# Four unread 4 MB transfers, in rows of 32 KB, in the load stream of a decode kernel

## The chip, the cores and the metric

The kernel runs on one core of one Trainium2 chip. The metric is the device time of one execution in microseconds (us). The time of a kernel is the median of its runs; the profile shows one execution, whose own span is a little shorter than its time.

## What is computed

One decode step: attention over the last 2048 of 8192 cached keys, mixed by a gate with a small MLP. There are 8 batches (B), 16 key/value heads (Hkv), 32 query heads, a head size of 128, a model size of 576, and all data is bf16.

```python
def reference(A_x, A_k_cache, A_v_cache, A_wq, A_wo, B_x, B_w1, B_b1, B_w2, B_b2, gate_w):
    def _A_ref(x, k_cache, v_cache, wq, wo):      # caches: [8, 16, 8192, 128]
        ...
        W = min(4096, max(256, Sk // 4))          # 2048
        q = (x @ wq).reshape(B, Sq, Hq, Dh).transpose(0, 2, 1, 3)
        k = jnp.repeat(k_cache[:, :, Sk - W:, :], rep, axis=1)
        v = jnp.repeat(v_cache[:, :, Sk - W:, :], rep, axis=1)
        scores = jnp.einsum("bhqd,bhkd->bhqk", q, k) * (Dh ** -0.5)
        o = jnp.einsum("bhqk,bhkd->bhqd", _softmax(scores), v)
        return o.transpose(0, 2, 1, 3).reshape(B, Sq, Hq * Dh) @ wo
    def _B_ref(x, w1, b1, w2, b2):
        h = _gelu(_layernorm(x) @ w1 + b1)
        return h @ w2 + b2
    x = A_x
    g = _sigmoid((x * gate_w).sum(-1, keepdims=True))
    return g * _A_ref(...) + (1 - g) * _B_ref(...)
```

The part of the caches that counts is 8 x 16 x 2048 x 128 x 2 B x 2, or 134 MB. The weights add another 20 MB.

## The kernel before

The kernel is a stream of loads with work hung on each. For each of the 16 key/value heads there is one K tile and one V tile, 4 MB each: all 8 batches, 2048 keys, 128 elements. `load_item` (line 602) issues such a load. It writes 128 partitions with two rows of 16 KB each, and reads the cache with the keys in 32 pieces of 64 outside and the batches inside. One pair of batch and head has 8192 keys of 256 B in the cache, so 2 MiB; neighbouring batches of the same head lie 32 MiB apart.

The list `stream` (lines 573 to 581) gives the order: K0, K1, K2, then V0, K3, V1, K4 and so on, after every fourth V tile a chunk of A_wo (`wo_chunk`, line 721), and at the end the bias and two groups of chunks of B_w2 (`m2_chunk`, line 738). In this text K8 is the K tile of head 8. Before the stream, A_wq and B_w1 are loaded for the query projection and the MLP's first layer.

All loads of the stream are issued by SyncE, in the order of the list: each has the one before it as its `after`. There are four slots of 32 KB a partition (`slot`, line 346), which `take_slot` (line 597) hands out in turn; the chunks of A_wo have a smaller fifth. A load waits until its slot is free, that is, until the last reader of the tile that lay there four tiles ago has finished. For a K tile (`k_unit`, line 641) the readers are four transposes on VectorE (line 649), behind each of which eight score matmuls on TensorE follow (lines 661 and, for those that keep their weights, 175). For a V tile (`v_item`, line 673) the reader is its product with the probabilities on TensorE (line 683). Two heads form a group; after the second K tile of a group comes its softmax (`softmax`, line 619: maximum on VectorE, exponent on ScalarE, transposed probabilities on VectorE), after its second V tile an evaluation on VectorE (lines 693 and 696).

Each engine runs its own list of instructions in order. These lists are made at build time by a planner (`_Plan.schedule`, line 62), which places each ready operation at the earliest time it can start by assumed durations, with 428 GB/s for loads. So a longer stream can also reorder work on other engines.

```python
        def load_item(cache, nm, hkv):
            s = take_slot()
            src = cache[:, hkv, S0:Sk, :].rearrange("b (x r) d -> x b (r d)", x=32)
            d = dma("sp", lambda e: e.dma_start(slot(s).rearrange("p (u n) -> p u n", u=2), src), "s%d" % s, 8 * W * Dh * 2, deps=slot_free[s], name="%s%d" % (nm, hkv), after=last_dma[-1:])
```

Of the kernel before, what the change touches and what calls it, by code (L numbers as in the profile page):

```python
# [38 lines left out]
class _Plan:  # L39
# [16 lines left out]
    def dma(self, eng, fn, semkey, nbytes, deps=(), name=None, after=(), prio=0):  # L56
        op = _Op(eng, fn, deps, name, self.DMA_ISSUE, after=after, is_dma=True, dma_sem=semkey, nbytes=nbytes, prio=prio)
        op.idx = len(self.all)
        self.all.append(op)
        return op  # L60
# [121 lines left out]
def build_kernel(nc, A_x, A_k_cache, A_v_cache, A_wq, A_wo, B_x, B_w1, B_b1, B_w2, B_b2, gate_w, out):  # L182
    B, Sq, D = A_x.shape
    _, Hkv, Sk, Dh = A_k_cache.shape
    Hq = A_wq.shape[1] // Dh
    F = B_w1.shape[1]
    W = min(4096, max(256, Sk // 4))
    assert Sq == 1 and Dh == 128 and B == 8 and W == 2048 and Hq == 2 * Hkv and Hkv == 16
    assert D == 576 and F == 4608
    S0 = Sk - W  # L190
# [19 lines left out]
    with ExitStack() as es:  # L210
# [135 lines left out]
        def slot(s):  # L346
            return RAW[:, s * DE:min((s + 1) * DE, ND * DE + SE)]
# [8 lines left out]
        def col(i, parts=128):  # L356
# [17 lines left out]
        add, dma = P.add, P.dma  # L374
# [7 lines left out]
                   deps=[o_idf], name="r8", cost=0.2)  # L382
# [19 lines left out]
        dx = [d_x, d_gw, d_gw1]  # L402
# [10 lines left out]
        for s in range(2):  # L413
            o_xz.append(add("dve", (lambda s=s: lambda e: e.tensor_copy(xz[:, s, :].rearrange("p (k z) -> p k z", z=2)[:, :, s], x_sb[:, 512:576]))(),  # L414
                            deps=dx + [o_xz0], name="xz%d" % s, cost=0.12))
# [12 lines left out]
        for s in range(2):  # L428
            o_yz.append(add("dve", (lambda s=s: lambda e: e.tensor_copy(yz[:, s, :].rearrange("p (k z) -> p k z", z=2)[:, :, s], y_bf[:, 512:576]))(),
                            deps=[o_y, o_yz0], name="yz%d" % s, cost=0.12))  # L430
# [142 lines left out]
        stream = [("K", 0), ("K", 1), ("K", 2)]  # L573
        for vi in range(Hkv):
            stream.append(("V", vi))
            if (vi + 1) % NVW == 0:
                stream.append(("W", vi // NVW))
            if vi + 3 < Hkv:
                stream.append(("K", vi + 3))
        M_CUTS = [[12, 12], [8, 3, 1]]  # L580
        stream += [("B", 0)] + [("M", i) for i in range(len(M_CUTS))]

        last_dma = [d_w1r]
        slot_free = [[o_qp], [], [], [o_hp], [o_qp, o_hp]]
# [12 lines left out]
        def take_slot():  # L597
            n = n_slot[0]
            n_slot[0] += 1
            return (1, 2, 0, 3)[n % ND]  # L600
# [5 lines that stand above are left out]
            last_dma.append(d)  # L606
            slot_free[s] = []
            return s, d

        def query(g):  # L610
            qb_done[g] = []
            for a in range(4):
                def fn(e, a=a):
                    dst = bass.AP(arena, offset=32 * a * AST + aoffs("qbd") + 32 * a, ap=[[AST, 32], [520, 4], [128, 4], [1, 8]])
                    src = bass.AP(arena, offset=32 * a * AST + aoffs("q4") + 32 * g, ap=[[AST, 32], [8, 4], [256, 4], [1, 8]])
                    return e.tensor_copy(dst, src)  # L616
                qb_done[g].append(add("pool", fn, deps=o_q4 + [o_qz, qk_unit.get(4 * g - 1)], name="qr%d_%d" % (g, a), cost=0.4))
# [54 lines left out]

        def v_item(hkv):
            s, d = load_item(A_v_cache, "dv", hkv)
            i = 2 * hkv + 1
            g, q = divmod(i, 4)
# [61 lines left out]
        def m2_chunk(ci):  # L738
            s = take_slot()
            j = sum(sum(c) for c in M_CUTS[:ci])  # L740
            at = 0
            src = B_w2.rearrange("(p j) n -> p (j n)", j=FT)
            ops = []
            for n, jn in enumerate(M_CUTS[ci]):
                d = dma("sp", (lambda j=j, jn=jn, at=at: lambda e: e.dma_start(slot(s)[:, at * D:(at + jn) * D], src[:, j * D:(j + jn) * D]))(),
                        "t%d" % (sum(len(c) for c in M_CUTS[:ci]) + n), 128 * jn * D * 2, deps=slot_free[s] if n == 0 else [], name="d_w2_%d_%d" % (ci, n), after=last_dma[-1:])
                last_dma.append(d)
# [8 lines left out]
        def k_item(hkv):  # L756
            s, d = load_item(A_k_cache, "dk", hkv)
            for u in range(2):
                k_unit(2 * hkv + u, s, d)
# [8 lines left out]
        pv_hist = []  # L768
        query(0)
        for kind, i in stream:  # L770
            {"K": k_item, "V": v_item, "W": wo_chunk, "M": m2_chunk, "B": bias}[kind](i)

        acc_ops = [g_.op for g_ in acc_groups]
        fin = []
# [34 lines left out]
def bass_gated_mix__sliding_block_cached__mixer_channel_mlp__decode_kernel(  # L809
    nc: bass.Bass,  # L810
    A_x: bass.AP,
    A_k_cache: bass.AP,
    A_v_cache: bass.AP,
    A_wq: bass.AP,
    A_wo: bass.AP,
    B_x: bass.AP,
    B_w1: bass.AP,
    B_b1: bass.AP,
    B_w2: bass.AP,
    B_b2: bass.AP,  # L820
    gate_w: bass.AP,
    out: bass.AP,
):
    build_kernel(nc, A_x, A_k_cache, A_v_cache, A_wq, A_wo, B_x, B_w1, B_b1, B_w2, B_b2, gate_w, out)
# [28 lines left out]
```

## Time and profile before

| what | value |
|---|---|
| median of 2 runs | 367.08 us (366.44 to 367.72) |
| the profiled execution | 366.56 us, of which span 364.7 us |
| TensorE matmuls, busy | 242.6 us (67% of the span) |
| VectorE, busy | 217.3 us (60%) |
| ScalarE / GpSimd, busy | 39.9 us / 23.2 us |
| moved by the DMA engines | 154.48 MB, mean 424 GB/s |
| 16 loads of K, 4096 KB each, median from issue to landing | 28.0 us |
| 16 loads of V, 4096 KB each, median from issue to landing | 32.6 us |

"Busy" is the time an engine spends in instructions. Loads are issued on SyncE's queue ("SPq") and run on the core's 16 DMA engines; the page gives their busy share (DMA, which rounds to a little over 1 when they are full) and what they move in GB/s. PE is TensorE, DVE VectorE, ACT ScalarE, POOL GpSimd, PEld TensorE's weight loads. L649 is line 649 of the kernel. The chain of waits follows the execution back from its last instruction: at each step to whatever released it, or to the instruction before it on its engine.

### The profile page before, as it was taken

Reading aid. Unit: us, or ns where it says so; the run is one execution under the profiler, and the core shown is the slowest. Engines: PE = TensorE matmul, PEld = TensorE weight load, DVE = VectorE, ACT = ScalarE, POOL = GpSimd, SP = SyncE. Lnnn points to the kernel's source line nnn. Section 1 sums busy time; section 2 is a strip of 40 time slices with the busy share of each in tenths; the row PEclk is TensorE's granted clock in tenths of the full one; section 3 lists DMA queues with packets and bytes.
Section 4 is the critical chain, followed back from the end, with each engine's and each line's share of the span. In section 5 each row is a group of like instructions: output and inputs, shape, how many; then the busy total and the mean of one; then the engine's idle time right before and its main releaser. Section 6 shows DMA issues by size and latency. Waiting matters only on the chain.

```text
span 364.7 us, 2619 instructions
## 1 busy us (share of the span) xinstructions
PE 242.6 (67%) x1329; PEld 57.0 (16%) x893; DVE 217.3 (60%) x160; ACT 39.9 (11%) x46; POOL 23.2 (6%) x66
## 2 busy tenths in 40 slices
PE   0346566599397956859197956868197948686675
PEld 0100000122011121202011121202011220102232
DVE  0722999666884757266774657276766668284220
ACT  1012100400400040000400040000400040002000
POOL 7210001000100100001000100001000100000000
PEclk9985599699979976969778976969798976989699
DMA  8999999999999999999999999999999999999995
GB/s 348 432 410 429 431 431 431 431 431 430 429 431 431 429 428 431 433 431 433 429 431 431 433 431 429 431 433 431 431 429 431 426 431 429 431 431 431 426 437 244
DMA packets 10675, 154.48 MB, mean 424 GB/s; under 512 B 764, under 2 KB 932, under 8 KB 1320
## 3 DMA queue, kind: packets, MB, share of 16 engines
q1 hardware_dynamic: 10608, 154.29, 99.0%
q8 instruction: 9, 0.15, 0.1%
q10 hardware_dynamic: 56, 0.03, 0.0%
q14 instruction: 2, 0.02, 0.0%
HBM read 154.31 MB, written 0.01 MB: 423 GB/s over the span
## 4 chain that ended last, share of the span: by engine, by line
DMA 58%; DVE 22%; PE 15%; issue 2%; ACT 1%; ACTq 0%; POOL 0%; DVEq 0%
DMA arena<-in_A_k_cache_dram 49%; DVE arena L649 18%; PE ps L175 9%; DMA arena<-in_B_w_dram 7%; PE ps L661 2%; DMA arena<-in_gate_w_dram 2%; PE ps L683 2%; PE ps L486 1%; DVE arena L548 1%; DVE arena L622 1%; ACT ps L631 1%; PE ps L565 0%; ACT arena L522 0%; DVE arena L543 0%; DVE arena L506 0%
## 5 line engine op out<-in xcount | busy, mean ns | idle before, releaser
L649 DVE STREAM_TRANSPOSE arena<-arena 128x2048 f32<-128x2048 f32 x64 | 144.5, 2291 | 60.0 <-DMA arena<-in_A_k_cache_dram 38.6
L175 PE MATMUL ps<-arena 128*128 128x512 bf16 (+2 forms) x453 | 136.3, 457 | 39.7 <-DVE arena L649 36.6
L683 PE MATMUL ps<-arena 128*32 128x512 bf16 x512 | 60.3, 390 | 3.1 <-DVE arena L637 2.0
L661 PE MATMUL ps<-arena 128*128 128x512 bf16 x114 | 50.5, 443 | 17.7 <-DVE arena L649 17.7
L626 ACT ACTIVATE arena<-ps,arena 128x2048 bf16<-128x2048 f32 x8 | 15.7, 1967 | 239.5 <-DVE arena L625 239.5
L661 PEld LDWEIGHTS ps<-arena 128*128 128x128 bf16 x128 | 13.9, 109 | 171.0 <-DVE arena L649 113.5
L683 PEld LDWEIGHTS ps<-arena 128*32 128x32 bf16 x512 | 25.1, 99 | 46.6 <-issue 20.4
L622 DVE TENSOR_REDUCE arena<-ps 128x1 f32<-128x2048 f32 x8 | 18.3, 2286 | 12.5 <-PE ps L175 12.4
L616 POOL COPY arena<-arena 32x128 bf16<-32x128 bf16 x32 | 9.2, 287 | 212.7 <-PE ps L175 202.9
L633 DVE STREAM_TRANSPOSE arena<-arena 128x2048 bf16<-128x2048 bf16 x8 | 18.3, 2291 | 6.4 <-ACT arena L626 6.4
L693 DVE SCALAR_TENSOR_TENSOR arena<-ps,arena 128x512 f32<-128x512 f32 x8 | 6.0, 752 | 20.2 <-PE ps L683 20.2
L565 PE MATMUL ps<-arena 128*8 128x288 bf16 (+1 forms) x140 | 12.6, 339 | 7.1 <-DVE arena L708 5.8
L702 PE MATMUL ps<-arena 128*128 128x256 f32 x16 | 5.6, 431 | 16.0 <-POOL arena L698 16.0
L635 PE MATMUL ps<-arena 128*128 128x1 f32 x16 | 4.5, 353 | 15.1 <-ACT ps L631 14.3
L631 ACT ACTIVATE ps<-arena 128x2048 f32<-128x2048 f32 x7 | 13.1, 1875 | 0.1
L698 POOL TENSOR_TENSOR arena<-arena 128x256 f32<-128x256 f32 x8 | 4.9, 612 | 109.4 <-DVE arena L625 61.7
L440 PE MATMUL ps<-arena 8*128 8x8 bf16 x8 | 0.6, 171 | 14.7 <-DVE arena L414 9.6
L696 DVE TENSOR_REDUCE arena<-arena 128x128 f32<-128x512 f32 x8 | 8.4, 1047 | 0.3
L565 PEld LDWEIGHTS ps<-arena 128*8 128x8 bf16 (+1 forms) x140 | 6.4, 97 | 13.5 <-DVE arena L708 7.0
L705 ACT ACTIVATE arena<-ps,arena 64x256 bf16<-64x256 f32 x8 | 3.7, 464 | 42.9 <-PE ps L702 42.8
L708 DVE STREAM_TRANSPOSE arena<-arena 128x256 bf16<-128x256 bf16 x4 | 2.5, 632 | 9.8 <-ACT arena L705 9.8
L543 DVE TENSOR_TENSOR arena<-arena 128x1152 f32<-128x1152 f32 x1 | 1.4, 1359 | 11.3 <-ACT arena L541 11.3
(86 smaller groups left out, 64.5 us busy)
## 6 DMA issues: line engine op xcount, KB each, us to landing
arena<-in_A_k_cache_dram SPq DMA_DIRECT2D x16, 4096.0 KB, 28.0
arena<-in_A_v_cache_dram SPq DMA_DIRECT2D x16, 4096.0 KB, 32.6
arena<-in_B_w_dram SPq DMA_DIRECT2D x1, 4608.0 KB, 23.4
arena<-in_A_wo_dram SPq DMA_DIRECT2D x4, 1152.0 KB, 34.1
arena<-in_A_wq_dram SPq DMA_DIRECT2D x1, 4096.0 KB, 12.9
arena<-in_B_w_dram SPq DMA_DIRECT2D x2, 1728.0 KB, 27.7
arena<-in_B_w_dram SPq DMA_DIRECT2D x1, 1152.0 KB, 27.1
arena<-in_B_w_dram SPq DMA_DIRECT2D x1, 576.0 KB, 24.3
```

What stands on the lines that cost most here:

```text
L175: return e.add_instruction(mybir.InstMatmult(name=nc.get_next_instruction_name(), engine=mybir.EngineType.PE, ins=[e.lower_ap(rhs), e.lowe ...
L565: ins = e.matmul(ps[32 * j:32 * j + 8, BK_ACC, 0:JN], lhsT, rhs[:, JN * j:JN * j + JN], start=False, stop=True, skip_group_check=True, til ...
L616: return e.tensor_copy(dst, src)
L622: mx = add("dve", lambda e: e.tensor_reduce(out=k(MX), in_=ps[:, 0:4, :].rearrange("p a n -> p (a n)"), axis=AXL.X, op=ALU.max), deps=[qk_ ...
L626: ex = add("act", lambda e: e.activation(out=Pm, in_=ps[:, 0:4, :].rearrange("p a n -> p (a n)"), func=ACTF.Exp, bias=k(NB), scale=SCALE, ...
L631: mask_done[g + 1] = add("act", lambda e: e.activation(out=ps[:, 0:4, :].rearrange("p a (n c) -> p (a n) c", c=4), in_=bass.AP(arena_f, of ...
L633: pt_done[g] = add("dve", lambda e: e.transpose(bass.AP(arena, offset=aoffs("PT") + 2048 * (g % 2), ap=[[AST, 128], [8, 64], [512, 4], [1, ...
L649: tr = add("dve", (lambda h=h, kb=kb: lambda e: e.transpose(bass.AP(arena_f, offset=foffs("KT") + kb * 2048, ap=[[AST // 2, 128], [1, 2048]]),
L661: mm = e.matmul(*args, start=False, stop=True, skip_group_check=True) if rc == 0 else held_matmul(nc, e, *args, stop=True, skip=True)
L683: mm = e.matmul(ps[c:c + 32, BK_OS[g % 2], :], PT[:, g % 2, 16 * c + 32 * t:16 * c + 32 * t + 32], slot(s)[:, (j % 2) * SE + 512 * t:(j % ...
L693: vmul = add("dve", lambda e: e.scalar_tensor_tensor(out=vmv, in0=ps[:, BK_OS[g % 2], :].rearrange("p (r d) -> p r d", r=4), scalar=rr[:, ...
L696: acc_ev[g] = add("dve", lambda e: e.tensor_reduce(out=EV[:, g % 2, :], in_=vm.rearrange("p (r d) -> p d r", r=4), axis=AXL.X, op=ALU.add) ...
```

## The change

Behind the K tiles of heads 8 and 11 in the stream, two more transfers each take the next slots in turn. Each moves 4 MB of the same caches: 32 pairs of batch and head (pairs 0 to 31 in the first two transfers, 64 to 95 in the other two, from A_k_cache and A_v_cache alternately), of each pair the first 512 of the last 2048 keys. The 128 KB of a pair go to four neighbouring partitions as four rows of 32 KB, which follow one another in the cache; the next pair begins 2 MiB further on. No operation reads what they bring. The slot is handed on when the transfer has landed.

```diff
@@ -577,6 +577,8 @@
                 stream.append(("W", vi // NVW))
             if vi + 3 < Hkv:
                 stream.append(("K", vi + 3))
+            if vi in (5, 8):
+                stream += [("X", 2 * (vi // 6)), ("X", 2 * (vi // 6) + 1)]
         M_CUTS = [[12, 12], [8, 3, 1]]
         stream += [("B", 0)] + [("M", i) for i in range(len(M_CUTS))]
@@ -606,6 +608,13 @@
             last_dma.append(d)
             slot_free[s] = []
             return s, d
+
+        def spare_item(n):
+            s = take_slot()
+            src = (A_k_cache, A_v_cache)[n % 2].rearrange("b h s d -> (b h) s d")[64 * (n // 2):64 * (n // 2) + 32, S0:S0 + 512, :].rearrange("j (x r) d -> j x (r d)", x=4)
+            d = dma("sp", lambda e: e.dma_start(slot(s), src), "s%d" % s, 8 * W * Dh * 2, deps=slot_free[s], name="dx%d" % n, after=last_dma[-1:])
+            last_dma.append(d)
+            slot_free[s] = [d]
@@ -768,7 +777,7 @@
         pv_hist = []
         query(0)
         for kind, i in stream:
-            {"K": k_item, "V": v_item, "W": wo_chunk, "M": m2_chunk, "B": bias}[kind](i)
+            {"K": k_item, "V": v_item, "W": wo_chunk, "M": m2_chunk, "B": bias, "X": spare_item}[kind](i)
```

The four transfers are called X0 to X3 below. In the lists of the engines, SyncE has four loads of 128 x 16384 elements more, X0 and X1 between K8 and V6, X2 and X3 between K11 and V9. TensorE, VectorE, ScalarE and GpSimd have the same instructions as before; on TensorE the products of V6, V9 and V10 and on VectorE the evaluation of V9's group have moved back by one to four places, and on ScalarE the mask of the sixth group stands before an output step and not behind it.

## The prediction

> **What bounds the kernel now.** I read the page's slices of the span first, then the table of stretches, the chain of waits, the queue of SyncE, and the row of the cache loads. The slices, each a fortieth of the span (9.1 us):
>
> ```profile
> DVE  0722999666884757266774657276766668284220
> DMA  8999999999999999999999999999999999999995
> GB/s 348 432 410 429 431 431 431 431 431 430 429 431 431 429 428 431 433 431 433 429 431 431 433 431 429 431 433 431 431 429 431 426 431 429 431 431 431 426 437 244
> ```
>
> The DMA engines are full from the second slice to the last but one and stay between 410 and 437 GB/s, while VectorE, the busiest helper in the loop, has room in most slices (60% of the span, TensorE 67%). The stretches sharpen this; the columns are the stretch, its length, the busy time of each engine, the clock, the DMA share and GB/s:
>
> ```profile
> 5.00:10.00 5.00, 0.41 (x7) 0.39 (x7) 0.81 (x3) 0.00 (x0) 2.90 (x3) 1.00 1.01 435
> ...
> 22.00:27.00 5.00, 1.89 (x7) 0.41 (x5) 1.10 (x1) 1.47 (x8) 1.15 (x4) 0.68 0.86 360
> ...
> 357.00:360.80 3.80, 2.46 (x29) 1.00 (x28) 0.00 (x0) 0.00 (x0) 0.00 (x0) 1.00 0.93 387
> 360.80:364.70 3.90, 1.71 (x24) 0.89 (x24) 0.45 (x1) 0.40 (x1) 0.00 (x0) 1.00 0.15 52
> ```
>
> Only the ends and one stretch near 25 us have free DMA time. In the middle, a stretch that begins where one wait for a K tile ends and stops where such a wait ends two groups of heads later, has none:
>
> ```profile
> 195.73:276.25 80.52, 55.49 (x281) 12.64 (x188) 50.19 (x32) 8.59 (x8) 3.52 (x10) 0.83 1.01 431
> ```
>
> In 80.5 us go four K tiles, four V tiles and one chunk of A_wo: 8 x 4.194 MB + 1.180 MB = 34.73 MB, and 34.73 MB / 80.52 us = 431.4 GB/s. The other three such stretches last 80.69, 80.69 and 80.46 us, so 430.4 to 431.7. VectorE works 50.2 of the 80.5 us. In the chain of waits the pieces are the same: after its transposes VectorE stands on the next K tile (start, length, what):
>
> ```profile
> 206.15 31.25 DMA arena<-in_A_k_cache_dram
> ...
> 248.71 27.51 DMA arena<-in_A_k_cache_dram
> ```
>
> The first number is when that tile was issued, so the issue came about 30 us, three tiles of 9.7 us, before the landing: the queue was two tiles deep when it went in. The row of the cache loads has the least and the most time from issue to landing:
>
> ```profile
> DMA to landing us min/median/max: 18.9/31.4/43.6
> ```
>
> Even the least, 18.9 us, is twice the 9.7 us of one tile. So SyncE waits a lot for free slots (212 us on the transposes in its own list of waits), but its next tile is always in the queue before the last one is through. The kernel is bound by bytes at 431 GB/s, with some 9 us of it at the ends.
>
> **The change, part by part.** It adds four DMA issues on SyncE's queue, X0 and X1 behind K8, X2 and X3 behind K11. It removes nothing.
>
> Bytes: each carries 32 x 512 x 128 x 2 B = 4.194 MB, so four are 16.78 MB. At the stretch's 431 GB/s that is 16.78 MB / 431 GB/s = 38.9 us. Nothing hides it: the stretches on both sides of K8 and K11 have a DMA share of 1.01, and all that follows in the stream moves back by it.
>
> Rate: no row has this pattern of reading, 128 rows of 32 KB where four follow one another and the next four begin 2 MiB on (a pair holds 8192 keys of 256 B). The nearest rows differ in one property each. The main load of A_wq also has 32 KB rows on 128 partitions, but without gaps; it lies in the stretch from 5 to 10 us, 435 GB/s. The K and V tiles have 16 KB rows and go through eight batches 32 MiB apart before they step to the next keys; they run at 431. So neither the long row nor a large step between neighbouring rows is dear by itself. What is new is that the two come together with places 2 MiB apart read at the same time. For bounds I take the highest rate of any stretch that I read (442 GB/s, 14 to 22 us: 38.0 us) and the lowest in which the loop's tiles were moving (the 360 GB/s above, which holds idle time too: 46.6 us). I choose 431, from the rows with the large step, which are nearest in their addresses: 38.9 us, between 38.0 and 46.6.
>
> The Trainium skill, page DMA: Bandwidth & Descriptors, section Latency and other measured facts, has a rule against this: copies of 128 rows of 16 KiB between HBM tensors ran at 207 GB/s in each direction at a row pitch of 512 KiB, 164 at 2 MiB and 103 at 4 MiB, where a padded pitch gave 214. By its 2 MiB figure the estimate is 38.9 x 214 / 164 = 50.8 us, by its 512 KiB figure (the mean pitch of a row here, four to a pair) 40.3 us. The K tiles' 32 MiB steps at 431 GB/s do not bear the rule out in its plain form, and no run here shows the pitch in question.
>
> Issue: four times 0.60 us on SyncE (its issues of cache tiles last 601 to 692 ns), beside a queue two tiles deep: nothing.
>
> Waits of the new transfers: X0 waits for the product of V4 and X1 for the transposes of K7, which V6 and K9 wait for now, in the same places; behind them on SyncE stand V6, K9 and all later loads. The chain gives the landing of K7 as 156.7 us (a piece of 32.75 us from 123.96 on), so V5 lands near 166.5, K8 near 176.2, X0 near 185.9 and X1 near 195.7, tile by tile of 9.7. The issues of now tell when each slot is free: V6's at 153.6 becomes X0's, K9's at 167.4 X1's, V7's at 173.0 (V5's product done) V6's, K10's at 191.0 (K8's transposes done) K9's. At 191.0 X1 and V6 still fill the queue until 205.4, so 14 us of it are left. V7 and K10 now wait for X0 and X1 themselves to land, near 186 and 196; nobody reads those, so their slots come free without transposes, and at 196 the queue holds V6, K9, V7 and a chunk of A_wo. Behind K11 it goes the same way: K11 lands near 256.9, X3 near 276.4, and K12 comes when K11's transposes are through, 11.3 us after its landing as now (248.7 against 237.4), with two tiles queued. No gap, so 0; were the queue to run dry once behind each pair, the price is a start from empty: the first load of A_wq, 0.52 MB, needed 3.6 us to landing where 431 GB/s would move it in 1.2, so 2.4 us, twice, 4.8 us.
>
> Order on the engines: TensorE does the product of V6 one half-tile later (behind K8's last score half, data already there), those of V9 and V10 behind score or softmax work of tiles that land earlier, and VectorE puts V9's evaluation behind the softmax steps of the group before. None of these now waits for a later tile. All lies beside 19.5 us of transfers that bring TensorE and VectorE no work, twice: 0. The cover for it is the 30 of 80.5 us in which VectorE is free.
>
> The tail: 36 tiles in place of 32 leave the order of the four slots as it was at the end, so the last loads and the 3.9 us behind them stay: 0.
>
> Sum: the profiled execution took 366.56 us (span 364.7 and 1.9 around it); 366.56 + 38.9 = 405.5. The two times shown have a median of 367.08, 0.5 more; 367.08 + 38.9 = 406.0. I take 405.8.
>
> **The rivals.**
>
> *Reads that collide.* The DMA engines, reading pairs 2 MiB apart in step, meet in the same part of the memory, and the four transfers run below the rest. For it: the loop's own tiles keep the engines on neighbouring keys, so the trace has never tried this. Against it: 32 MiB steps at 431 GB/s, and 128 KB in a row at each place. Mild, from the 360 GB/s above to three quarters of 431 (323): 46.6 to 51.9 us, 413 to 418.5. Strong, half of 431: 77.9 us, 444.5. It decides from about 415 GB/s down, where the four last over 40.4 us. The skill's rule named above is this rival; its 2 MiB figure gives an estimate of 417.4, its 4 MiB figure 447.
>
> *The queue runs dry* behind each pair, because V7 and K10 wait for a transfer rather than for compute: 4.8 us more, 410.5. Against it are the three tiles queued at K10's issue.
>
> *Not slower.* The four transfers find room that the DMA engines have, beside K and V tiles that leave it unused; the place is the stretch from V5's landing to K13's. The free DMA time that the stretches show is 1.0 us before 5 us, 0.7 near 25, and 0.3 + 3.3 behind 357, together 5.3 us and none of it at that place. To stay within 2% (7.3 us) 16.78 MB would have to pass at 2,300 GB/s, over five times the highest rate seen; it decides only if the tiles' share there fell well below 1. Or the transfers don't move all they name; but four issues with 128 x 16384 elements stand in SyncE's order. Faster than before needs a gain beyond the 38.9 us, and the free time is only 5.3.
>
> **How the numbers follow.** Full rate, no gap: 0.66, 404 to 408 (442 GB/s at 404.6 less half a microsecond between executions; 415 GB/s and the higher median at 407.5). Queue dry: 0.08, near 410.5. Mild collision: 0.16, 413 to 418.5. Strong collision: 0.08. Not slower: 0.02. The range from 404 to 418 takes in the first three but for their edges, some 0.85; stopping short of the mild collision would leave out a quarter. Over 2%, which is about what a measurement of this kernel can tell from no change, lies at 374.4: slower has 0.98, within 0.015, faster 0.005.
>
> **What would show it.** In the changed profile: 171.3 MB in the queue of the loads; slices at 431 GB/s without a dip at the two places, about 176 to 196 us and 257 to 276 us; two stretches of some 19.5 us in which TensorE and VectorE have little to do; the chain's share of K loads up by about 39 us; an unchanged tail. A dip of the slices at a DMA share near 1 speaks for colliding reads; a dip with a lower share for a dry queue. The forecast is wrong if the four transfers together take under 37 or over 41 us of the DMA engines.

## The result, and the profile after

The changed kernel takes 405.55 us (two runs, 405.33 and 405.78) against 367.08: a ratio of 1.1055, 95% interval 1.1031 to 1.1079. The forecast was 405.8 in a range of 404 to 418. The profiled execution took 405.33 us with a span of 403.5 us, which is 38.8 us more span than before; the sum had said 38.9.

The slices of the span of the changed kernel, now of 10.1 us each:

```profile
DVE  1526997487856654568005666562073666556311
DMA  8999999999999999999999999999999999999996
GB/s 363 411 428 427 432 432 430 432 431 429 432 432 429 426 439 430 430 441 442 413 432 427 432 434 432 447 432 419 430 430 427 431 435 432 427 432 432 429 427 262
```

The DMA row looks as it did: full from the second slice to the last but one. The rate is where it was. At the two places of the new transfers it reads 441, 442, 413 and 447, 432, 419; each three together have a mean of 432 or 433, so these are most likely bytes booked a slice early or late and no dip. The two stretches in which the new transfers run say the same; the columns are those of the prediction's table:

```profile
176.20:195.70 19.50, 10.26 (x36) 1.62 (x12) 11.39 (x6) 3.77 (x4) 0.19 (x1) 0.82 0.99 426
256.90:276.40 19.50, 8.88 (x36) 1.56 (x12) 13.91 (x9) 3.94 (x3) 1.14 (x4) 0.86 1.00 432
```

The 426 GB/s of the first follow 437 in the 19.5 us before it (156.73 to 176.20 us), and both together have 431. VectorE, on the other hand, has three slices at 0, the 20th and 21st (192 to 212 us) and the 29th (282 to 292 us): the unread transfers bring it nothing. The queue of the loads (packets, MB, share), before and after, from the pages, and the time from issue to landing of the four transfers, from the row of their line:

```profile
q1 hardware_dynamic: 10608, 154.29, 99.0%
```

```profile
q1 hardware_dynamic: 11184, 171.07, 99.1%
```

```profile
DMA to landing us min/median/max: 25.4/29.7/34.4
```

171.07 MB less the 154.29 of before are 16.78 MB, four full transfers. They needed 25.4 to 34.4 us from issue to landing, so each went into a queue that held about two tiles before it, as K and V tiles do. Next the stretches behind the new transfers, two later ones for comparison:

```profile
195.70:237.40 41.70, 20.71 (x103) 5.18 (x80) 14.39 (x11) 3.41 (x4) 1.75 (x5) 0.75 1.01 431
...
276.40:315.00 38.60, 20.72 (x98) 5.09 (x74) 10.80 (x6) 0.47 (x1) 0.61 (x1) 0.71 1.01 430
315.00:355.00 40.00, 29.96 (x148) 6.79 (x102) 25.48 (x16) 4.41 (x4) 1.75 (x5) 0.79 1.01 431
...
399.50:403.50 4.00, 1.72 (x24) 0.91 (x24) 0.45 (x1) 0.40 (x1) 0.00 (x0) 1.00 0.15 51
```

In the first two, which begin where X1 and X3 have landed, VectorE (the third engine column) works 14.4 of 41.7 and 10.8 of 38.6 us, where a stretch of that length further on (the third line) gives it 25.5 of 40. The DMA share stays 1.01 in these three. The last line is the tail, as long and as empty as before. The chain of waits, in order of time:

```profile
190.88 24.27 DMA arena<-in_A_k_cache_dram
...
250.74 25.41 DMA arena<-in_A_v_cache_dram
276.16 38.86 DMA arena<-in_A_k_cache_dram
```

The second piece is X3, issued at 250.74 and landed at 276.15; the forecast had 276.4. The third is K13, issued the moment X3 landed and itself landed at 315.0, where it landed at 276.25 before: later by 38.8 us, all of the loss. Nothing further is lost or won behind it. In the list of waits of SyncE's queue stands the wait that is new:

```profile
SPq L607 <- DMA arena<-in_A_v_cache_dram: 12.0, 2, 9.1
```

The issues of K10 and K13 waited 12.0 us in all for X1 and X3 to land; the DMA engines were full all the while, so this wait cost nothing.

### The profile page after: what moved, and what is told of

Its sections match the earlier page's. It is cut to its first block, busy times and chain, and to the rows that moved or that the text cites. A ratio compares the mean times of both kernels' runs of the same rounds, so it can differ in the third digit from the quotient of the medians.

```text
span 403.5 us, 2641 instructions
## 1 busy us (share of the span) xinstructions
PE 256.0 (63%) x1347; PEld 59.3 (15%) x893; DVE 217.6 (54%) x160; ACT 40.1 (10%) x46; POOL 23.2 (6%) x66
## 3 DMA queue, kind: packets, MB, share of 16 engines
q1 hardware_dynamic: 11184, 171.07, 99.1%
## 4 chain that ended last, share of the span: by engine, by line
DMA 53%; DVE 22%; PE 20%; ACT 3%; issue 2%; ACTq 0%; POOL 0%; DVEq 0%
DMA arena<-in_A_k_cache_dram 38%; DVE arena L658 17%; PE ps L175 10%; DMA arena<-in_B_w_dram 7%; DMA arena<-in_A_v_cache_dram 6%; PE ps L692 4%; PE ps L670 3%; DMA arena<-in_gate_w_dram 2%; PE ps L565 1%; PE ps L486 1%; ACT ps L640 1%; ACT arena L635 1%; DVE arena L548 1%; DVE arena L631 1%; DVE arena L705 1%
## 5 line engine op out<-in xcount | busy, mean ns | idle before, releaser
L670 PE MATMUL ps<-arena 128*128 128x512 bf16 x128 | 58.6, 458 | 54.3 <-DVE arena L658 54.1
L692 PE MATMUL ps<-arena 128*32 128x512 bf16 x512 | 65.3, 413 | 25.9 <-DMA arena<-in_A_v_cache_dram 23.9
L692 PEld LDWEIGHTS ps<-arena 128*32 128x32 bf16 x512 | 26.5, 104 | 72.1 <-DMA arena<-in_A_v_cache_dram 25.7
L633 PE MATMUL ps<-arena 128*128 128x4 f32 x16 | 3.5, 289 | 6.6 <-DVE arena L632 6.6
```

The source lines that it names most:

```text
L670: mm = e.matmul(*args, start=False, stop=True, skip_group_check=True) if rc == 0 else held_matmul(nc, e, *args, stop=True, skip=True)
L692: mm = e.matmul(ps[c:c + 32, BK_OS[g % 2], :], PT[:, g % 2, 16 * c + 32 * t:16 * c + 32 * t + 32], slot(s)[:, (j % 2) * SE + 512 * t:(j % ...
```

## The experiments

All kernels compute the whole result; only the unread transfers differ. "Extra" is the median less the median of the kernel before, run beside it on the same chip. The theory is that the 38.9 us are bytes at the stream's rate and nothing else. Rivals: the pattern of reading has a price that something else gave back; each transfer, or each break in the prefetch, has a price of its own; and reads that collide.

**The changed kernel again**, as a base for the others. No edit.

> The changed kernel again, so that the runs beside it stand against it on the same chip. Bytes theory (16.78 MB more at the stream's 431 GB/s, nothing hidden, nothing else): 38.9 us over the kernel before, 405.5 to 406.0 us, ratio 1.106. If the first result was luck of one chip, more than 1.5 us off.

405.31 us (405.14 to 405.57), ratio 1.1041 (1.1022 to 1.1061), extra 38.4 us.

**The pattern of a K tile.**

```diff
-            src = (A_k_cache, A_v_cache)[n % 2].rearrange("b h s d -> (b h) s d")[64 * (n // 2):64 * (n // 2) + 32, S0:S0 + 512, :].rearrange("j (x r) d -> j x (r d)", x=4)
-            d = dma("sp", lambda e: e.dma_start(slot(s), src), ...
+            src = (A_k_cache, A_v_cache)[n % 2][:, 4 * n, S0:Sk, :].rearrange("b (x r) d -> x b (r d)", x=32)
+            d = dma("sp", lambda e: e.dma_start(slot(s).rearrange("p (u n) -> p u n", u=2), src), ...
```

> The four transfers read as a K tile does (one head, all batches, 16 KB rows, steps of 32 MiB) instead of 32 pairs in rows of 32 KB; still unread, same places, same bytes. Bytes theory: the same time as the changed kernel within 0.7 us, about 405.5. Pattern theory (the 2 MiB steps cost something, and something else, such as the rest that the compute engines get, gave it back): shorter than the changed kernel by what the pattern costs, 1.5 us or more, so under 404; or longer if the long rows gained.

405.84 us (405.58 to 406.13), ratio 1.1056 (1.1036 to 1.1076), extra 38.9 us. The pattern of the change costs nothing beside the loop's own; what difference there is, 0.5 us, favours it. That a price of the pattern was given back elsewhere is out.

**All 128 rows 2 MiB apart.**

```diff
-            src = ...[64 * (n // 2):64 * (n // 2) + 32, S0:S0 + 512, :].rearrange("j (x r) d -> j x (r d)", x=4)
+            src = ...[:, S0 + 128 * (n // 2):S0 + 128 * (n // 2) + 128, :].rearrange("p s d -> p (s d)")
```

> The four transfers read 128 keys of each of all 128 pairs: each of the 128 rows of 32 KB begins 2 MiB after the one before, none follows another directly. Bytes theory: 405.5 us, rate 431 GB/s in the two places. Collision theory, with the rule of the Trainium skill (DMA: Bandwidth & Descriptors, Latency and other measured facts) taken at its 2 MiB figure: 50.8 us for the four in place of 38.9, 417 us, and slices of the transfers near 330 GB/s at a full DMA share.

406.59 us (406.07 to 406.74), ratio 1.1072 (1.1048 to 1.1095), extra 39.6 us: 1.3 us over the changed kernel, not the 12 of the collision theory. The Trainium skill's figure for 2 MiB, which the expectation takes up, doesn't hold for this load.

**Half the bytes.**

```diff
-... S0:S0 + 512, :] ...
+... S0:S0 + 256, :] ...
-            d = dma("sp", lambda e: e.dma_start(slot(s), src), "s%d" % s, 8 * W * Dh * 2, ...
+            d = dma("sp", lambda e: e.dma_start(slot(s)[:, 0:SE], src), "s%d" % s, 4 * W * Dh * 2, ...
```

> The four transfers take 256 keys of each pair instead of 512, rows of 16 KB, 2 MB each: 8.39 MB in all. Bytes theory: 19.5 us over the kernel before, 386.0 to 386.5 us. Theory of a fixed price for each transfer or each pair of transfers (a stop of the queue, a break in the prefetch) that makes up part of the 38.9 us: more than 19.5 by half of that price; with the dry queue's 4.8 us in the 38.9 it would be 21.9 us, 389.

386.75 us (385.86 to 387.26), ratio 1.0533 (1.0509 to 1.0557), extra 19.8 us; the upper end of the interval is 20.4. A fixed price as large as the dry queue's, by which the extra would have been 21.9, is out. A smaller one, up to 1.8 us for the four (twice what 20.4 is above 19.5), this run leaves open.

**Eight transfers.**

```diff
-            if vi in (5, 8):
-                stream += [("X", 2 * (vi // 6)), ("X", 2 * (vi // 6) + 1)]
+            if vi in (2, 5, 8, 11):
+                stream += [("X", 2 * (vi // 3)), ("X", 2 * (vi // 3) + 1)]
...
-            src = ...[64 * (n // 2):64 * (n // 2) + 32, ...
+            src = ...[32 * (n // 2):32 * (n // 2) + 32, ...
```

> Eight such transfers instead of four, in pairs behind K5, K8, K11 and K14, 33.55 MB more. Bytes theory: 77.8 us over the kernel before, 444.7 us. Theory that part of the 38.9 us was hidden and another part a price of its own (a dry queue): the hidden part would not double, so off by 2 us or more either way.

444.24 us (444.05 to 445.62), ratio 1.2104 (1.2072 to 1.2137), extra 77.3 us. Twice the bytes, twice the time (2 x 38.4 = 76.8): no fixed part of the 38.9 us was hidden and none was paid once. A price of each transfer would have doubled too; for that the half dose stands.

**Four in a row.**

```diff
-            if vi in (5, 8):
-                stream += [("X", 2 * (vi // 6)), ("X", 2 * (vi // 6) + 1)]
+            if vi == 8:
+                stream += [("X", n) for n in range(4)]
```

> All four behind K11, one behind another, so that the compute engines get nothing for 39 us and all four slots are taken by unread data. Bytes theory: the same 405.4 us as the changed kernel, within 0.7 us, since the queue still holds three transfers when each slot comes free. Theory of a dry queue (each later load waits for a transfer to land rather than for compute): 2.4 us or more for each stop of the queue, 408 us or above. Theory that the rest for the compute engines costs something by itself (TensorE restarts at a lower clock and later work falls behind): more than the changed kernel's too, without a fall of the DMA share.

405.34 us (405.2 to 405.51), ratio 1.1036 (1.1007 to 1.1065), extra 38.4 us, the same as in two pairs, and the DMA row of its slices is full from the second to the last but one. A rest of 39 us for the compute engines, and slots that come free by a landing, cost nothing.

**64 places 4 MiB apart, two rows at each.**

```diff
+            src = (A_k_cache, A_v_cache)[n % 2].rearrange("b h s d -> (b h) s d").rearrange("(j z) s d -> j z s d", z=2)[:, n // 2, S0:S0 + 256, :].rearrange("j (x r) d -> j x (r d)", x=2)
```

> The four transfers read 256 keys of every second pair: 64 places 4 MiB apart, two rows of 32 KB at each, same bytes. Bytes theory, with the 1.3 us that the 2 MiB rows took more than the changed kernel (four transfers 40.2 us instead of 38.9) as its limit: 405.3 to 406.6 us. Collision theory, by the larger step: more than the 2 MiB rows' 406.6, and with the Trainium skill's 4 MiB figure (DMA: Bandwidth & Descriptors, Latency and other measured facts) an estimate of 447 us.

426.31 us (425.8 to 428.42), ratio 1.1619 (1.158 to 1.1658), extra 59.4 us: 21 us more for the same bytes. So colliding reads exist in this kernel. Its slices:

```profile
DMA  8999999999999999999999999999999999999996
GB/s 348 432 423 434 423 440 424 436 426 434 431 429 434 429 432 432 377 288 259 389 434 426 434 432 438 313 253 289 426 437 426 431 429 435 428 434 431 432 427 259
```

At the two places the rate falls to 259 and 253 while the DMA share stays full: the engines are at work and move less. That is what a dip of this kind looks like, and in the changed kernel's slices there is none. Idle DMA engines lower both: the stretch from 22 to 27 us of the kernel before has a share of 0.86 at 360 GB/s.

**16 places 16 MiB apart, eight rows at each.**

```diff
+            src = (A_k_cache, A_v_cache)[n % 2].rearrange("b h s d -> (b h) s d").rearrange("(j z) s d -> j z s d", z=8)[:, n // 2, S0:S0 + 1024, :].rearrange("j (x r) d -> j x (r d)", x=8)
```

> The four transfers read 1024 keys of every eighth pair: 16 places 16 MiB apart, 256 KB in a row at each (eight rows of 32 KB), same bytes. If each of the 16 DMA engines takes one place, all read in step at addresses that differ by multiples of 16 MiB alone. Bytes theory: 405.3 to 406.6 us. Collision theory: clearly more, 415 us or above, since no engine is ever on neighbouring keys of another.

449.22 us (448.49 to 452.05), ratio 1.2246 (1.2197 to 1.2295), extra 82.3 us. The slices:

```profile
DMA  8999999999999999999999999999899999999995
GB/s 354 439 413 433 429 432 432 427 430 432 426 430 438 427 436 350 214 219 208 350 435 424 437 432 366 217 202 225 306 432 429 432 429 435 427 430 436 427 430 227
```

Half the rate, 202 to 225 GB/s, at a full DMA share. And yet at each place 256 KB lie in a row, the most of any run until then. It is not that some engines stop: in the trace the 512 packets of 32 KB of the four transfers took 2.54 us in the median and none under 1.7, where those of the changed kernel took 1.21.

**4 MiB apart, four rows at each**, and **2 MiB apart, two rows at each**, to part the step from the stay.

```diff
+            src = ...rearrange("b h s d -> (b h) s d").rearrange("(j z) s d -> j z s d", z=2)[32 * (n // 2):32 * (n // 2) + 32, 0, S0:S0 + 512, :].rearrange("j (x r) d -> j x (r d)", x=4)
...
+            src = ...rearrange("b h s d -> (b h) s d")[64 * (n // 2):64 * (n // 2) + 64, S0:S0 + 256, :].rearrange("j (x r) d -> j x (r d)", x=2)
```

> As the changed kernel (32 places, four rows of 32 KB in a row at each), but every second pair, so that the places lie 4 MiB apart instead of 2 MiB. One property differs. If the step between places decides: near the 426 us of the run with 4 MiB steps and two rows, 420 us or above. If the shorter stay at each place (64 KB instead of 128 KB) made that run slow: 405 to 407 us.

408.32 us (407.43 to 409.46), ratio 1.1128 (1.1102 to 1.1155), extra 41.6 us.

> 64 neighbouring pairs, two rows of 32 KB in a row at each: as the run with 4 MiB steps and two rows, but 2 MiB apart. If the step decides: 405 to 407 us. If the number of rows in a row decides: near 426 us.

407.82 us (407.16 to 409.38), ratio 1.1119 (1.1091 to 1.1147), extra 41.1 us.

Neither is where the step alone or the stay alone would have put it (405 to 407 or over 420): neither decides by itself. Each alone adds some 3 us to the changed kernel, both together 21.

**16 MiB apart, shifted by 4 KiB from place to place**, and **by 32 KiB** (from key 4096 on, so that all places stay in their pairs).

```diff
+            src = bass.AP((A_k_cache, A_v_cache)[n % 2].tensor, offset=(n // 2) * Sk * Dh + S0 * Dh, ap=[[8 * Sk * Dh + 16 * Dh, 16], [128 * Dh, 8], [1, 128 * Dh]])
...
+            src = bass.AP((A_k_cache, A_v_cache)[n % 2].tensor, offset=(n // 2) * Sk * Dh + 4096 * Dh, ap=[[8 * Sk * Dh + 128 * Dh, 16], [128 * Dh, 8], [1, 128 * Dh]])
```

> As the run with 16 places 16 MiB apart and eight rows of 32 KB at each, but each place begins 16 keys (4 KiB) further on in its pair than the one before. Theory that equal low address bits of places read in step make the reads collide: back to 405 to 408 us. Theory that the distance itself is dear (many far regions at once): 449 us again. The Trainium skill (DMA: Bandwidth & Descriptors, Latency and other measured facts) has 4 KiB of padding bring back the full rate at a 4 MiB pitch, so by it 405 us.

450.14 us (447.91 to 451.07), ratio 1.2253 (1.2209 to 1.2297), extra 83.4 us.

> As the run with 16 places 16 MiB apart, eight rows of 32 KB at each, but each place begins 128 keys (32 KiB) further on than the one before; the offsets below 16 MiB are then those of neighbouring keys, as in a K tile. If equal offsets (over more than 4 KiB) of places read in step make the reads collide: back to 405 to 408 us. If the distance of 16 MiB itself is dear: 449 us again, like the run with 4 KiB.

449.05 us (448.97 to 450.09), ratio 1.2249 (1.222 to 1.2278), extra 82.3 us.

No shift helps. My theory that the reads collide because places read in step have equal low addresses falls, at least for shifts of 4 and 32 KiB.

## Why the prediction was right, point by point

- **Bytes at the stream's rate.** 16.78 MB at 431 GB/s, 38.9 us; measured 38.5 (405.55 - 367.08), and 38.4 again. Half the bytes cost 19.8 us, twice the bytes 77.3. Shown by three doses that lie on one line within 1 us.
- **Nothing hides it.** Shown by the same doses, and by the DMA share of 1.01 in the stretches before and after.
- **The rate of the new pattern.** The step from rows that were near (32 KB rows without gaps, 32 MiB steps with 16 KB rows) to 431 GB/s came out right, and the K tile's own pattern takes the same time. But the reasoning was weaker than its result, and that this term fitted was in part luck. "Neither the long row nor a large step is dear by itself" said little of the two together, and the runs show layouts of the same 4 MB, in the same 32 KB rows, that cost up to twice as much. The rival, reads that run below the stream's rate at a full DMA share, was real, though what they collide on is not shown; the change lies on its cheap side. Its price for the strong form, half the rate and 444.5 us, is near what 16 places gave (449.2); the price for the mild form, 413 to 418.5, lies between the runs that lost 3 us and the one that lost 21.
- **The queue.** K9's issue was forecast at 191.0 and came at 190.88, K10's near 196 and at 195.68. V7 was said to follow X0's landing near 186 and came at 191.54: it stands behind K9 on SyncE, which I had in the list but left out of its time. X1, V6 and K9 were queued, so it cost nothing. K12's issue came 8.9 us after K11's landing (265.68 against 256.76) and not 11.3, also without an effect. Four transfers in a row, with all slots freed by landings, show that the queue doesn't run dry.
- **Order on the engines.** Nothing to see in the time: K13 and the tail are both late by 38.8 us.
- **Two signs were wrong.** The rest of the compute engines was said to lie beside the transfers, from 176 to 196 us; but beside them VectorE works 11.4 and 13.9 of 19.5 us, as K8 and K11 had just landed. The rest came mostly after them, in the slices from 192 and from 282 us on. And the chain's K loads did not grow by 39 us: they fell from 49% of 364.7 to 38% of 403.5 us, 179 to 153, with 25 us of V loads beside them, while TensorE's share went from 15 to 20%. The chain passes from a load to whatever freed its slot, also where the load then only stands in the queue, so it tells which operations can be linked and not what the time is made of. The DMA row of the slices and the stretches carried this case.

A rule of the Trainium skill (DMA: Bandwidth & Descriptors, Latency and other measured facts), that copies between HBM tensors slow down at row pitches of 2 MiB and more and that 4 KiB of padding restores a pitch of 4 MiB, agrees with these loads in part only: at 128 rows 2 MiB apart the four took 39.6 us where an estimate by its figure is 50.8, at 4 MiB with two rows 59.4 where it is 80.8, and 4 KiB more between places 16 MiB apart, of eight rows each, changed nothing (82.3 to 83.4). No run here pads every row, and none copies within HBM.

## What to carry to other kernels

In this kernel, where the DMA share is full in nearly every slice and the rate is flat, added bytes cost bytes over rate even when nobody reads them, and the rest that the compute engines got gave nothing back. The rate depended on the layout that was read, and the size of the rows alone did not tell it: the same rows of 32 KB ran between 201 and 437 GB/s. So before a load is laid out anew, run the new pattern as an unread transfer in the old stream, and look for a fall of GB/s at a full DMA share. A pattern that is near a fast one in each single property can still be slow.

## What the runs showed of the hardware that was not expected

The same four transfers, 16.78 MB in rows of 32 KB, by where they read (GB/s is 16.78 MB over the extra time; the unread transfers of the kernel with K tile pattern, rows of 16 KB, took 38.9):

| places | step between them | in a row at each | extra, us | GB/s |
|---|---|---|---|---|
| 32 (the change) | 2 MiB | 128 KB | 38.4 | 437 |
| 128 | 2 MiB | 32 KB | 39.6 | 423 |
| 64 | 2 MiB | 64 KB | 41.1 | 408 |
| 32 | 4 MiB | 128 KB | 41.6 | 404 |
| 64 | 4 MiB | 64 KB | 59.4 | 283 |
| 16 | 16 MiB | 256 KB | 82.3 | 204 |
| 16 | 16 MiB + 4 KiB | 256 KB | 83.4 | 201 |
| 16 | 16 MiB + 32 KiB | 256 KB | 82.3 | 204 |

No single column orders the last one: 64 places are fast at 2 MiB and slow at 4, a step of 4 MiB is fast with 32 places and slow with 64, and 128 places over the same 256 MiB as the slow ones are fast. A guess that fits: if each of the 16 DMA engines takes blocks of neighbouring rows, say of eight, these blocks begin 4 MiB apart in the change, 8 MiB in the two runs at 41 us and 16 MiB in the others; among those at 16 MiB, the more places one block passes through (8, 4, 1), the better it goes (39.6, 59.4, 82.3). Blocks of four halve these distances (with 16 places, two of them then share a place) and give the same order. No run shows which engine reads which row, so this is only argued, and what it is in the memory that the reads share stays open.
